# Channel mixing of two batches: six hidden blocks summed in a PSUM bank per addition, in place of three

## The chip, the cores and the metric

One NeuronCore of a Trainium2 chip runs the whole program; the other cores are idle. The metric is the device time of one execution in microseconds, median of the runs, smaller is better. TensorE (PE) multiplies into PSUM, VectorE (DVE) and ScalarE (ACT) read and write PSUM and SBUF, GpSimd (POOL) works on SBUF, and SyncE (SP) issues all DMA transfers.

## The reference

Attention over four batches of 448 rows with 12 heads of 64, then a mixer (over the rows, then over the channels), then a gated mixer. The change touches the channel mixing alone:

```python
x = attention(q, k, v)                                # (4, 448, 768)
xt = x.transpose(0, 2, 1)
u = x + (np.maximum(xt @ w_tok1, 0.0) @ w_tok2).transpose(0, 2, 1)
h2 = np.maximum(u @ w_ch1, 0.0) @ w_ch2               # 768 -> 1536 -> 768
x = u + h2
...
```

## The kernel before

Each product of fp32 precision is made of three matmuls on split operands (mm3, L332): each operand is a rounded high part and a low part, and high x high, high x low and low x high are summed in PSUM. Everything is transposed: U[b] holds channels on the partitions, in six blocks of 128 by 448 rows.

**What runs when.** Every instruction of the kernel is a job with an engine, a duration, a list of what it reads and writes and a priority. The class Plan (order, due, run; L134 to L270) plays the jobs through, engine by engine, six times with changing priorities, and the order of starts in the best pass is the order in which the program is written. Each engine then works strictly in that order. A change in one function can so move instructions of all others.

The attention of the 24 head pairs is in the front half: scores (L497, tile pss), masked reduction on DVE (L506), exponential on ACT (L523), normalisation on POOL (L544), transposes on PE (L581, pst), weighting (L683 and L688, pso); after each three pairs follows half a batch of row mixing (psm). The channel mixing of batches 0 and 1 is laid between these, from about 70 to 400 us; batches 2 and 3 are done in another way after 402 us (tile psf).

**The weights of channel mixing** arrive as 64-bit numbers. They are cut into 24 blocks, listed in UNITS: (1, f) is the part of w_ch1 that makes hidden block f of 128 channels, (2, q, e) the part of w_ch2 that takes hidden blocks 3q to 3q+2 to output blocks 2e and 2e+1. The place in this list is called position here, 0 to 23. convert (L375) loads a block into one of the way buffers (L381), narrows it on DVE in two halves of three steps each (narrow, L340; L351, L353, L355; tile psw), and stores it to DRAM as tile plain (L395). load_unit (L814) brings a block back (L818), casts its high part on ACT (L819) and makes the low part on POOL (lo_part, L327), in one of four buffers w0 to w3, by position modulo 4 (tile whl; the first three positions are split without the detour). Batch 1 loads the same 24 blocks again. The weights of the later gated mixer go the same way in tile gw (L1105, L1107), with the same narrowing steps on DVE.

**The two products.** ch1 (L831) takes a block of w_ch1: three jobs of six matmuls into a bank (tile ps, 18 matmuls), a relu on ACT (L843) into hid, and on DVE the remainder of the relu (relu_lo, L330), the low part of hid; this empties the bank. Six hid buffers h0 to h5 hold hidden blocks, by f modulo 6. ch2 (L846) takes a block of w_ch2: for each of its two output blocks, nine matmuls over three hidden blocks into a bank (tile ps again) and an addition of the bank into U on DVE (L859). Both products share two banks, 6 and 7 (banks_c, L791). In the program's order the tiles of both are told apart as ps1 and ps2.

Before the change the list runs: three of w_ch1, then four times three of w_ch1 (as long as there are any) and three of w_ch2. So a second product follows its hidden blocks with three other blocks between.

Of the kernel before, what the change touches and what calls it, by code (L numbers as in the profile page):

```python
# [16 lines left out]
B, H, S, D = 4, 12, 448, 64  # L17
# [6 lines left out]
NF = CH // 128  # L24
FF = 512
NG = FF // 128
HALF = 384
# [1 line left out]
MASKED = -8.0e9  # L29


UNITS = [(1, f) for f in range(3)]
for q in range(4):
    UNITS += [(1, f) for f in range(3 * q + 3, min(3 * q + 6, NF))] + [(2, q, e) for e in range(3)]
LN_EPS = 1e-6

DIRECT = tuple(range(3))
# [60 lines left out]
class Plan:  # L98
# [11 lines left out]
    def job(self, eng, us, emit, r=(), w=(), touch=(), prio=0.0, at=0.0, size=0, port=False, other=None):  # L110


        j = Job(eng, us, emit, prio, at, size, len(self.jobs), port, other)
        for k in r:
            if k in self.writer:
                j.before.add(self.writer[k])
            self.readers.setdefault(k, []).append(j)
        for k in w:
            if k in self.writer:
                j.before.add(self.writer[k])  # L120
            j.before.update(self.readers.get(k, ()))
            self.writer[k] = j
            self.readers[k] = []
        j.before.discard(j)
        for k in (*r, *w):
            if isinstance(k[0], Buf):
                j.bufs.add(k[0])
        for b in j.bufs:
            b.jobs.append(j)
        j.bufs |= set(touch)  # L130
        self.jobs.append(j)
        return j
# [146 lines left out]
def mixer_kernel(ctx: ExitStack, tc: tile.TileContext, qkv, wtok, wch, wgv, wsp, bsp, out):  # L279
# [19 lines left out]
    job = plan.job  # L299

    def buf(tag, shape, dtype, name):
        return plan.buf(tag, lambda t: sb.tile([128, *shape], dtype, tag=t, name=name))
# [6 lines left out]
    def bank(banks, name):  # L309
        return Buf(lambda i: psp.tile([128, 512], F32, tag=f"b{i}", name=name), None, banks=banks)  # L310
# [5 lines left out]
    def dve(n, psum=True):  # L316
        return (n * 1.05 + 60) / 1e3 if psum else (n * 1.09 + 40) / 1e3
# [14 lines left out]
    def mm3(ps, terms, first=True, last=True, **kw):  # L332

        n = len(terms)
        for i, (ah, al, bh, bl) in enumerate(terms):
            nc.tensor.matmul(ps, ah, bh, start=(first and i == 0), stop=False, **kw)  # L336
            nc.tensor.matmul(ps, ah, bl, start=False, stop=False, **kw)  # L337
            nc.tensor.matmul(ps, al, bh, start=False, stop=(last and i == n - 1), **kw)  # L338
# [63 lines left out]
    LOW = 1e5  # L402
# [147 lines left out]
    def u_keys(b, d):  # L550
        return [(U[b], d, 0), (U[b], d, 1)]
# [164 lines left out]
    mixed = {}  # L716
# [76 lines left out]
    WU = {}  # L793
# [28 lines left out]
    def split_u(b, ts, prio):  # L822
        u = U[b]
        for k in range(KM):
            t, i = ts[k // 3], k % 3
            job("ACT", act(S, False), lambda k=k, t=t, i=i: nc.scalar.copy(t.t[:, i, 0, :], u.t[:, k, :]), r=u_keys(b, k), w=[(t, i, 0)], prio=prio)
            job("POOL", pool(S), lambda k=k, t=t, i=i: lo_part(nc.gpsimd, t.t[:, i, 1, :], u.t[:, k, :], t.t[:, i, 0, :]), r=[*u_keys(b, k), (t, i, 0)], w=[(t, i, 1)], prio=prio)

    hidden = {}
# [14 lines left out]
        job("DVE", dve(S), lambda: relu_lo(h.t[:, 1, :], ps.t[:, :S], h.t[:, 0, :]), r=[(ps, 0), (h, 0)], w=[(h, 1)], prio=-1)  # L844

    def ch2(b, q, e, i):  # L846
        w = WU[b, i]
        u = U[b]
        hs = [hidden[b, 3 * q + f] for f in range(3)]
        for dd in range(2):  # L850
            d = 2 * e + dd
            ps = bank(banks_c, "ps2")

            def mms(dd=dd, ps=ps):
                cs = [slice(HALF * dd + 128 * f, HALF * dd + 128 * f + 128) for f in range(3)]
                mm3(ps.t[:, :S], [(w.t[:, 0, c], w.t[:, 1, c], h.t[:, 0, :], h.t[:, 1, :]) for c, h in zip(cs, hs)])

            job("PE", 1.82, mms, r=[*((w, 0, c) for c in range(2)), *((h, x) for h in hs for x in range(2))], w=[(ps, 0), ("mixed", b, d)], prio=LOW + 24 * b + i)
            job("DVE", dve(S), lambda d=d, ps=ps: nc.vector.tensor_tensor(u.t[:, d, :], ps.t[:, :S], u.t[:, d, :], op=ALU.add), r=[(ps, 0), *u_keys(b, d)], w=u_keys(b, d), prio=-1)  # L859

    def channel(b):
        xs = [buf(f"X{k}", [3, 2, S], F32R, "uhl") for k in range(2)]
        split_u(b, xs, -0.5)
        for i, u in enumerate(UNITS):
            if b:
                load_unit(b, i)
            if u[0] == 1:
                ch1(b, u[1], i, xs)
            else:
                ch2(b, u[1], u[2], i)  # L870

    everything = list(range(8))
# [167 lines left out]
    def channel_pair(b0, b1):  # L1040

        index = {u: i for i, u in enumerate(UNITS)}
        us = (U[b0], U[b1])
# [109 lines left out]
    for k in range(KM):  # L1153
        w, h, l = singles[k % 2], *value_w[k // 3 * 2 : k // 3 * 2 + 2]
        job("SP", 0.4, lambda k=k, w=w: nc.sync.dma_start(w.t, gated_w[8 + k]), r=[("gated", 8 + k)], w=[(w, 0)], prio=LOW + VALUE_PRIO + k, size=262144)
        job("ACT", act(FF, False), lambda k=k, w=w, h=h: nc.scalar.copy(h.t[:, k % 3, :], w.t), r=[(w, 0)], w=[(h, k, 0)], touch=[l], prio=LOW + VALUE_PRIO + k)  # L1156
        e, name, us = (nc.vector, "DVE", dve(FF, False)) if k in VALUE_DVE else (nc.gpsimd, "POOL", pool(FF))
# [122 lines left out]
    for i in range(2):  # L1280
        job("SP", 0.4, lambda i=i: nc.sync.dma_start(sp_in[i].t, wsp[:, 2 * S * i : 2 * S * i + 2 * S].rearrange("p (c s) -> p c s", c=2)), w=[(sp_in[i], 0)], prio=LOW + 130, size=458752)
        for c in range(2):
            w = sp_w[2 * i + c]
# [153 lines left out]
def _layout(inputs):  # L1437
# [34 lines left out]
    second = c2.reshape(4, 3, 128, 3, 2, 128).transpose(0, 3, 2, 4, 1, 5).reshape(4, 3, 128, DM)  # L1472
    wch = np.concatenate([first[u[1]] if u[0] == 1 else second[u[1], u[2]] for u in UNITS], axis=1)
    wi = inputs["moe2_w_in"]
# [33 lines left out]
```

## Time and profile before

| | us |
|---|---|
| median of 3 runs | 760.47 |
| the runs | 758.69, 760.47, 761.64 |
| span of the profiled execution | 760.7 |
| busy: PE, DVE, ACT, POOL | 747.2, 622.3, 427.4, 298.2 |
| chain that ended last: share of PE, of DVE | 9%, 2% |

The profiled execution's own time is given by its span alone; it stands 0.2 us over the median. The busy share of PE counts matmuls from their start to a modelled end; two that follow each other overlap, so the idle time of PE is what the table of waits shows, and the rate is seen in the starts of the timeline. The granted clock of PE is given per stretch, 1.00 for full speed.

### The profile page before, as it was taken

How to read it: one execution, taken by the hardware profiler on the slowest of the kernel's cores; microseconds unless marked ns; L12 is line 12 of the kernel's file. 1: busy time of each engine (PE TensorE's matmuls, PEld its weight loads, DVE VectorE, ACT ScalarE, POOL GpSimd, SP SyncE). 2: the span in 40 equal slices, each digit the busy share in tenths (PEclk: the TensorE clock that was granted, in tenths of full speed). 3: DMA queues.
4: the chain of work that ended last, by engine and by line, in shares of the span. 5: the costliest groups of instructions: out<-in, count | busy, mean ns of one | idle time of the engine just before them, and what ended most of it. 6: DMA issues, size and time to landing. Idle time of an engine off the chain costs nothing. (4 is left out here: it accounts for less than half of the span.)

```text
span 760.7 us, 12440 instructions
## 1 busy us (share of the span) xinstructions
PE 747.2 (98%) x4216; PEld 640.3 (84%) x4216; DVE 622.3 (82%) x1512; ACT 427.4 (56%) x1040; POOL 298.2 (39%) x354
## 2 busy tenths in 40 slices
PE   8999999999989999999999999999999999999998
PEld 4577778888887888888889989998988888888997
DVE  6999599999867878876469978999999897599482
ACT  6998776445347765552336666654573665545241
POOL 4788764265494766563310000000420151542210
PEclk9999999999999999999999999999999999999999
DMA  6687158999976898898823122520301100400213
GB/s 228 207 285 238 55 163 316 335 318 333 339 225 190 298 307 250 234 304 220 241 84 117 39 84 84 187 84 1 118 22 42 43 0 1 132 1 28 83 49 133
DMA packets 48608, 122.02 MB, mean 160 GB/s; under 512 B 4896, under 2 KB 20256, under 8 KB 48032
## 3 DMA queue, kind: packets, MB, share of 16 engines
q1 hardware_dynamic: 48544, 121.23, 48.7%
q8 instruction: 33, 0.54, 0.3%
q14 instruction: 31, 0.25, 0.1%
HBM read 91.46 MB, written 29.75 MB: 159 GB/s over the span
## 5 line engine op out<-in xcount | busy, mean ns | idle before, releaser
L336 PE MATMUL psf<-fb,fa 128*128 128x448 f32 x420 | 154.0, 367 | 1.2 <-DVE hs L1001 0.6
L337 PE MATMUL psf<-fb,fa 128*128 128x448 f32 x420 | 153.7, 366 | 0.0
L338 PE MATMUL psf<-fb,fa 128*128 128x448 f32 x420 | 153.6, 366 | 0.0
L327 POOL TENSOR_TENSOR whl<-whl 128x768 fp32r<-128x768 f32 x45 | 83.2, 1851 | 89.5 <-ACT whl L819 89.4
L523 ACT ACTIVATE P<-P,stats 128x448 f32<-128x448 f32 (+3 forms) x192 | 96.1, 505 | 31.1 <-DVE stats L506 30.8
L544 POOL TENSOR_SCALAR P<-P,stats 128x448 f32<-128x448 f32 (+3 forms) x192 | 88.3, 483 | 38.1 <-DVE stats L535 30.8
L336 PEld LDWEIGHTS psf<-fb,fa 128*128 128x128 f32 x420 | 78.9, 188 | 9.2 <-DVE hs L1001 1.0
L337 PEld LDWEIGHTS psf<-fb,fa 128*128 128x128 f32 x420 | 78.9, 188 | 6.8
L338 PEld LDWEIGHTS psf<-fb,fa 128*128 128x128 f32 x420 | 78.9, 188 | 6.7
L506 DVE CUSTOM_DVE_ANT_0 P<-pss,mask 128x448 f32<-128x448 f32 (+3 forms) x192 | 70.9, 415 | 16.4 <-PE pss L497 16.0
L938 ACT CAST fa<-raw 128x384 fp32r<-128x384 f32 (+1 forms) x112 | 56.4, 531 | 42.7 <-DVE raw L951 21.6
L327 POOL TENSOR_TENSOR wv<-wf,wv 128x512 fp32r<-128x512 f32 x6 | 9.2, 1546 | 153.2 <-ACT wv L1156 153.2
L327 DVE TENSOR_TENSOR fa<-raw,fa 128x384 fp32r<-128x384 f32 (+1 forms) x109 | 61.0, 585 | 7.1 <-ACT fa L938 7.1
L336 PE MATMUL ps<-hid,whl 128*128 128x448 f32 x144 | 55.2, 383 | 3.1 <-DVE hid L330 1.9
L819 ACT CAST whl<-whl 128x768 fp32r<-128x768 f32 x45 | 37.4, 833 | 34.6 <-DMA whl<-plain 33.5
L336 PE MATMUL ps<-uhl,whl 128*128 128x448 f32 x144 | 55.6, 386 | 0.2 <-DVE U L859 0.2
L338 PE MATMUL ps<-hid,whl 128*128 128x448 f32 x144 | 53.3, 370 | 0.0
L337 PE MATMUL ps<-hid,whl 128*128 128x448 f32 x144 | 53.3, 370 | 0.0
L338 PE MATMUL ps<-uhl,whl 128*128 128x448 f32 x144 | 52.7, 366 | 0.0
L337 PE MATMUL ps<-uhl,whl 128*128 128x448 f32 x144 | 52.7, 366 | 0.0
L859 DVE TENSOR_TENSOR U<-ps,U 128x448 f32<-128x448 f32 x48 | 29.5, 619 | 20.9 <-PE ps L338 20.8
L327 POOL TENSOR_TENSOR ql<-stage,qh 128x896 fp32r<-128x896 f32 x18 | 38.1, 2116 | 14.9 <-issue 11.7
(174 smaller groups left out, 1793.2 us busy)
## 6 DMA issues: line engine op xcount, KB each, us to landing
way<-in_wch SPq DMA_DIRECT2D x24, 768.0 KB, 5.7
whl<-plain SPq DMA_DIRECT2D x45, 384.0 KB, 5.0
stage<-in_qkv SPq DMA_DIRECT2D x23, 448.0 KB, 4.7
plain<-way SPq DMA_DIRECT2D x24, 384.0 KB, 6.7
raw<-plain SPq DMA_DIRECT2D x24, 384.0 KB, 3.9
round<-PB SPq DMA_DIRECT2D x7, 1024.0 KB, 6.2
PT<-round SPq DMA_DIRECT2D x28, 256.0 KB, 6.2
v<-in_qkv SPq DMA_DIRECT2D x24, 256.0 KB, 4.1
```

Source lines behind the costliest of these rows:

```text
L327: e.tensor_tensor(lo, x, hi.bitcast(F32), op=ALU.subtract)
L336: nc.tensor.matmul(ps, ah, bh, start=(first and i == 0), stop=False, **kw)
L337: nc.tensor.matmul(ps, ah, bl, start=False, stop=False, **kw)
L338: nc.tensor.matmul(ps, al, bh, start=False, stop=(last and i == n - 1), **kw)
L506: nc.vector.tensor_tensor_reduce(out=P(i)[:M, j, :], in0=ps(i, j), in1=mask[:M, S - 128 : S - 128 + W] if j == 0 and n < BLOCKS or M == 64 ...
L523: nc.scalar.activation(P(i)[:M, j, :], P(i)[:M, j, :], AF.Exp, bias=s.t[:M, 0, c : c + 1], scale=-1.0, accum_out=s.t[:M, 1, c : c + 1])
L544: nc.gpsimd.tensor_scalar(P(i)[:M, j, :], P(i)[:M, j, :], s.t[:M, 2, c : c + 1], 1.0, op0=ALU.mult, op1=ALU.mult)
L819: job("ACT", act(DM, False), lambda: nc.scalar.copy(w.t[:, 0, :], w.t[:, 1, :].bitcast(F32)), r=ks, w=ks, prio=p)
L859: job("DVE", dve(S), lambda d=d, ps=ps: nc.vector.tensor_tensor(u.t[:, d, :], ps.t[:, :S], u.t[:, d, :], op=ALU.add), r=[(ps, 0), *u_keys( ...
L938: job("ACT", act(n, False), lambda: nc.scalar.copy(part(o, 0), at(d)), r=[key(d)], w=[wk], prio=p + 0.1 * o)
```

## The change

The list now runs six of w_ch1, six of w_ch2, and the same again. Within the six of w_ch2 the blocks that serve the same output blocks stand in pairs: (2, 0, e) and (2, 1, e), then the next e. ch2 is called once for a pair and takes both weight blocks: a bank gets nine matmuls with the first block (hidden blocks 0 to 2 of the six) and nine with the second (hidden blocks 3 to 5), as two jobs, and one addition into U follows the eighteen. Per batch there are so 12 banks of 18 matmuls and 12 additions for the second product instead of 24 banks of nine and 24 additions. The host lays the blocks out in the new order. Batches 2 and 3 use the same blocks by another index and are otherwise as before.

```diff
-UNITS = [(1, f) for f in range(3)]
-for q in range(4):
-    UNITS += [(1, f) for f in range(3 * q + 3, min(3 * q + 6, NF))] + [(2, q, e) for e in range(3)]
+UNITS = []
+for x in range(2):
+    UNITS += [(1, f) for f in range(6 * x, 6 * x + 6)] + [(2, q, e) for e in range(3) for q in (2 * x, 2 * x + 1)]
...
     def ch2(b, q, e, i):
-        w = WU[b, i]
+        w = [WU[b, i - 1], WU[b, i]]
         u = U[b]
-        hs = [hidden[b, 3 * q + f] for f in range(3)]
         for dd in range(2):
             d = 2 * e + dd
             ps = bank(banks_c, "ps2")
...
+            for x in range(2):
+                hs = [hidden[b, 3 * (q - 1 + x) + f] for f in range(3)]
...
+                    mm3(ps.t[:, :S], [(w[x].t[:, 0, c], w[x].t[:, 1, c], h.t[:, 0, :], h.t[:, 1, :]) for c, h in zip(cs, hs)], first=x == 0, last=x == 1)
...
             job("DVE", dve(S), lambda d=d, ps=ps: nc.vector.tensor_tensor(u.t[:, d, :], ps.t[:, :S], u.t[:, d, :], op=ALU.add), r=[(ps, 0), *u_keys(b, d)], w=u_keys(b, d), prio=-1)
...
-            else:
+            elif u[1] % 2:
                 ch2(b, u[1], u[2], i)
```

The change moves instructions on every engine, since the plan is made anew. Two places show it. The first is VectorE ahead of the relu remainder of position 17 (the last of w_ch1 in both lists), whose bank is wanted by a second product of position 18. Before, from the second half of position 22 on (way2 holds even positions, way3 odd ones; psw is the bank that the narrowing steps share):

```order
L351 TENSOR_SCALAR psw_2636<-way2_156 128x384
L353 SCALAR_TENSOR_TENSOR psw_2636<-way2_156,psw_2636 128x384
L355 SCALAR_TENSOR_TENSOR way2_156<-way2_156,psw_2636 128x384
L330 SCALAR_TENSOR_TENSOR hid_2631<-ps1_2585,hid_2631 128x448
L351 TENSOR_SCALAR psw_2658<-way3_158 128x384
L353 SCALAR_TENSOR_TENSOR psw_2658<-way3_158,psw_2658 128x384
L355 SCALAR_TENSOR_TENSOR way3_158<-way3_158,psw_2658 128x384
L330 SCALAR_TENSOR_TENSOR hid_2677<-ps1_2622,hid_2677 128x448
```

And now, from the first half of position 21 on:

```order
L351 TENSOR_SCALAR psw_2487<-way3_158 128x384
L353 SCALAR_TENSOR_TENSOR psw_2487<-way3_158,psw_2487 128x384
L355 SCALAR_TENSOR_TENSOR way3_158<-way3_158,psw_2487 128x384
L330 SCALAR_TENSOR_TENSOR hid_2499<-ps1_2446,hid_2499 128x448
L351 TENSOR_SCALAR psw_2520<-gw_1948 128x384
L353 SCALAR_TENSOR_TENSOR psw_2520<-gw_1948,psw_2520 128x384
L355 SCALAR_TENSOR_TENSOR gw_1948<-gw_1948,psw_2520 128x384
L584 COPY PT_2518<-pst_2524 128x448
L351 TENSOR_SCALAR psw_2544<-way3_158 128x384
L353 SCALAR_TENSOR_TENSOR psw_2544<-way3_158,psw_2544 128x384
L355 SCALAR_TENSOR_TENSOR way3_158<-way3_158,psw_2544 128x384
L330 SCALAR_TENSOR_TENSOR hid_2558<-ps1_2490,hid_2558 128x448
```

The relu remainder of position 17 stood behind the first half of position 23; it now stands behind the second half of position 21.

The second place is TensorE, where a weight buffer is used up and the block four positions on is wanted. Before, the closest such places are positions 14 to 18: whl_2372 is position 14, whl_2561 is position 18 in the same buffer; shown are the last matmul on the one and the first matmuls of the others.

```order
L338 MATMUL ps2_2537<-hid_2012,whl_2372 128x448
...
L336 MATMUL ps1_2554<-uhl_864,whl_2427 128x448
...
L336 MATMUL ps1_2585<-uhl_864,whl_2489 128x448
...
L336 MATMUL ps1_2622<-uhl_864,whl_2516 128x448
...
L336 MATMUL ps2_2667<-hid_2285,whl_2561 128x448
```

Now it is positions 8 to 12: whl_1920 is position 8, whl_2006 position 9, whl_2077 and whl_2114 are 10 and 11, and whl_2184 is position 12, in the buffer of position 8. Shown are the last matmul on position 8 and the first of each nine that follow:

```order
L338 MATMUL ps2_2159<-hid_1703,whl_1920 128x448
L336 MATMUL ps2_2159<-hid_1825,whl_2006 128x448
...
L336 MATMUL ps2_2189<-hid_1458,whl_2077 128x448
...
L336 MATMUL ps2_2189<-hid_1825,whl_2114 128x448
...
L336 MATMUL ps2_2222<-hid_1458,whl_2077 128x448
...
L336 MATMUL ps2_2222<-hid_1825,whl_2114 128x448
...
L336 MATMUL ps1_2257<-uhl_864,whl_2184 128x448
```

Between the last use of a buffer and the first use of the block that follows in it stood three blocks of 18 matmuls; at this place now stand five times nine.

## Rows read from the trace of the kernel before

**Rows 1.** The page's head and part 1: busy us (share of the span) xinstructions

```profile
span 760.7 us, 12440 instructions
...
PE 747.2 (98%) x4216; PEld 640.3 (84%) x4216; DVE 622.3 (82%) x1512; ACT 427.4 (56%) x1040; POOL 298.2 (39%) x354
```

**Rows 2.** Table of waits, TensorE: us in total, times, longest us

```profile
PE ps L336 <- DVE hid L330: 1.9, 1, 1.9
...
PE ps L336 <- DVE U L859: 1.2, 2, 1.1
```

**Rows 3.** Table by stretch: length, busy us (xinstructions) by engine, PE clock, DMA share, GB/s

```profile
180.00:200.00 20.00, 18.68 (x96) 16.02 (x95) 18.39 (x44) 7.69 (x18) 8.07 (x7) 1.00 0.94 332
200.00:220.00 20.00, 18.07 (x84) 16.28 (x83) 14.49 (x31) 10.55 (x19) 14.90 (x15) 0.91 0.85 287
...
214.00:216.00 2.00, 2.00 (x7) 1.76 (x7) 1.93 (x5) 1.88 (x4) 2.00 (x3) 0.50 0.57 219
```

**Rows 4.** Timeline of TensorE, 192 to 217 us: start, us, instruction [idle before <-releaser]

```profile
194.91 0.47 PE L336 MATMUL ps<-hid,whl 128*128 128x448 f32 x1 [1.05 <-DVE U L859]
...
212.13 0.47 PE L336 MATMUL ps<-hid,whl 128*128 128x448 f32 x1 [1.94 <-DVE hid L330]
...
213.04 0.51 PE L337 MATMUL ps<-hid,whl 128*128 128x448 f32 x1
...
216.63 0.36 PE L338 MATMUL ps<-hid,whl 128*128 128x448 f32 x1
216.83 0.36 PE L336 MATMUL ps<-hid,whl 128*128 128x448 f32 x1
```

**Rows 5.** Timeline of VectorE, 192 to 212 us

```profile
192.58 0.56 DVE L351 TENSOR_SCALAR psw<-gw 128x384 uint32<-128x384 uint32 x1 [0.92 <-DMA gw<-in_wgv]
...
194.24 0.62 DVE L859 TENSOR_TENSOR U<-ps,U 128x448 f32<-128x448 f32 x1
...
209.07 0.56 DVE L351 TENSOR_SCALAR psw<-way 128x384 uint32<-128x384 uint32 x1 [1.15 <-DMA way<-in_wch]
...
210.98 0.56 DVE L355 SCALAR_TENSOR_TENSOR way<-way,psw 128x384 uint32<-128x384 uint32 x1 [0.75 <-DMA plain<-way]
211.45 0.62 DVE L330 SCALAR_TENSOR_TENSOR hid<-ps,hid 128x448 fp32r<-128x448 f32 x1
```

**Rows 6.** VectorE by line, 100 to 215 us: xcount | busy us, mean ns | idle before

```profile
L353 DVE SCALAR_TENSOR_TENSOR psw<-way,psw 128x384 uint32<-128x384 uint32 x38 | 21.3, 561 | 1.2
...
L506 DVE CUSTOM_DVE_ANT_0 P<-pss,mask 128x192 f32<-128x192 f32 (+3 forms) x33 | 12.6, 413 | 0.1
L859 DVE TENSOR_TENSOR U<-ps,U 128x448 f32<-128x448 f32 x13 | 7.8, 616 | 0.0
```

**Rows 7.** Timeline of TensorE, 94 to 103 us: half a score, weighting, transposes

```profile
94.80 0.47 PE L497 MATMUL pss<-qh 64*128 64x448 f32 x2
...
95.75 0.85 PE L741 MATMUL psm<-ident,U 128*64 128x128 f32 x6
...
100.10 0.97 PE L683 MATMUL pso<-PT,v 128*64 128x448 f32 x4
...
102.32 0.66 PE L581 MATMUL pst<-ident,P 128*128 128x128 f32 x4
```

**Rows 8.** Timeline of SyncE's queue: block loads of positions 12, 18 and 20

```profile
164.36 0.32 SPq L818 DMA_DIRECT2D whl<-plain  x1
...
197.44 0.38 SPq L818 DMA_DIRECT2D whl<-plain  x1
...
204.81 0.32 SPq L818 DMA_DIRECT2D whl<-plain  x1
```

**Rows 9.** Timeline of GpSimd: splits of positions 12, 18, and 20 with 21

```profile
171.00 1.85 POOL L327 TENSOR_TENSOR whl<-whl 128x768 fp32r<-128x768 f32 x1
...
206.47 1.86 POOL L327 TENSOR_TENSOR whl<-whl 128x768 fp32r<-128x768 f32 x1
...
215.32 3.63 POOL L327 TENSOR_TENSOR whl<-whl 128x768 fp32r<-128x768 f32 x2
```

More of the change, by code (lines that the diff above doesn't have):

```diff
@@ L852, in ch2, with mms @@
             ps = bank(banks_c, "ps2")
[L854 to L858, printed above, removed]
+            for x in range(2):
+                hs = [hidden[b, 3 * (q - 1 + x) + f] for f in range(3)]
+                def mms(dd=dd, ps=ps, x=x, hs=hs):
+                    cs = [slice(HALF * dd + 128 * f, HALF * dd + 128 * f + 128) for f in range(3)]
+                    mm3(ps.t[:, :S], [(w[x].t[:, 0, c], w[x].t[:, 1, c], h.t[:, 0, :], h.t[:, 1, :]) for c, h in zip(cs, hs)], first=x == 0, last=x == 1)
+                job("PE", 1.82, mms, r=[*((w[x], 0, c) for c in range(2)), *((h, y) for h in hs for y in range(2))], w=[(ps, 0), ("mixed", b, d)], prio=LOW + 24 * b + i)
             job("DVE", dve(S), lambda d=d, ps=ps: nc.vector.tensor_tensor(u.t[:, d, :], ps.t[:, :S], u.t[:, d, :], op=ALU.add), r=[(ps, 0), *u_keys(b, d)], w=u_keys(b, d), prio=-1)
```

## The prediction

> **What bounds the kernel now.** The page's first part comes first: the span and the busy share of each engine [rows 1]. TensorE is busy 747.2 of 760.7 us, so there is little to win anywhere: a change that leaves the number of matmuls alone can only move the 13.5 us in which TensorE stands still, and what its clock loses. This change leaves all 864 matmuls of channel mixing for batches 0 and 1 in place. The second view is the table of waits for TensorE alone [rows 2]: two of its three longest entries are in channel mixing (tile ps), 1.9 us for VectorE's hid and 1.2 us for VectorE's U (the other stands at the kernel's start, which the change leaves alone). The third view is the table by stretch [rows 3]: both lie between 180 and 220 us, where TensorE is busy 18.68 and 18.07 of 20 us, and from 200 to 220 us its granted clock averages 0.91. Nothing else in the middle of the kernel stands out.
>
> The timeline of TensorE shows the two places [rows 4]. At 194.91 a second product begins 1.05 us late, behind an addition (L859) on VectorE. At 212.13 the next one begins 1.94 us late, behind the relu remainder (L330). Neither waits for its own operands: both need one of the two PSUM banks of channel mixing, which VectorE has not emptied yet. VectorE's timeline says why [rows 5]. At 192.58 VectorE had stood idle 0.92 us for a load of gw, with the addition that frees the bank three instructions behind it. At 209.07 it had stood 1.15 us for a load of way, at 210.98 another 0.75 us for a store of plain, and the relu remainder that frees the bank (211.45) is the very next instruction. So the cause is the order on VectorE: narrowing of weights that has not arrived sits ahead of the instruction that frees a bank, and a bank that is filled in nine matmuls leaves only nine matmuls of time.
>
> **What one such wait costs.** A matmul's row ends 0.36 us after its start while the next starts 0.20 us after it (the rows at 216.63 and 216.83 [rows 4]), so a wait costs 0.16 us more than the idle time shown. Idle time in channel mixing there: 1.05 at 194.91, 1.94 at 212.13, and about 0.2 for the rest of the 1.2 us that rows 2 put down to U: 3.2 us in three waits, with 3 x 0.16 = 0.5 it is 3.7 us. After the longest of them the matmuls get slower: from 213.04 to 216.63 ten of them take 3.59 us instead of 10 x 0.203 = 2.03 us [rows 4], which is the dip of the granted clock in rows 3: 0.50 from 214 to 216 us, the lower of its two levels, 1.2 GHz. That adds 1.6 us. The whole place costs 5.3 us.
>
> **The change part by part.** *Additions.* 48 additions into U become 24: 24 x 0.616 us = 14.8 us less on VectorE [rows 6]. By itself this is worth nothing, because VectorE is not what ends; it counts only through what stands behind an addition in VectorE's order.
>
> *Time to empty a bank.* A bank of the second product is filled by 18 matmuls (3.7 us) in place of 9 (1.83 us). Where the order runs bank after bank, VectorE has twice the time for the other one. Where both banks are open at once (positions 18 to 21 of batch 0) the first is closed nine matmuls ahead of the second, so the margin is that of before, 1.83 us plus what attention puts between.
>
> *VectorE's order at the place of the long wait.* In both kernels it follows position 17, the last block of the first product. Ahead of its relu remainder VectorE now has 6 additions instead of 12 (6 x 0.62 = 3.7 us less), three narrowed half blocks less (each three steps of 0.56 us [rows 6], some 0.55 to 0.6 from start to start: 5.0 us) and one attention score block of 8 masked reductions less (8 x 0.38 = 3.1 us by the group's 12.6 us over 33 [rows 6]), with the small steps around it about 12.8 us less in all. TensorE reaches the place earlier as well: one pair's scores, four transposes and the weighting of one pair are now behind it, which by their rows is 2 x 0.95 + 0.4 + 2.2 = 4.5 us [rows 7]; I count 4.8 with the change of kind between them. VectorE's lead over TensorE therefore grows by 12.8 - 4.8 = 8 us, against a wait of 1.94 us. The narrowing steps ahead of it belong to position 21, no longer to 22 and 23, and the load of position 21 stands on SP right behind the block load of position 17, which waits until position 13 is used up, some 20 us of matmuls ahead of this place. Summed along both orders with the durations of this trace, the lead of the freeing instruction over the matmul that needs the bank is smallest at this very place before (4.8 us, and 5.2 to 5.8 around the other two waits); afterwards it is nowhere under 11 us. I take all three waits as gone: 760.7 - 3.7 - 1.6 = 755.4 us.
>
> *Weight buffers.* This is the term that speaks against the change. Four buffers hold the split weight blocks, and a second product now needs two at once. A buffer can be loaded again when its block is used up, and the new block must be loaded (SP), cast (ScalarE) and split (GpSimd) before its turn. Before, the shortest such interval is 54 matmuls, 11.0 us (positions 16 to 19). Now it is 45 matmuls, 9.2 us, at position 12, and 10.4 us at position 14. What the way takes is read from load issue to the end of the split: position 12 of before 164.36 to 172.85, 8.5 us; position 18 197.44 to 208.33, 10.9 us [rows 8, 9]. Bounds for the new wait: nothing by the first, 10.9 - 9.2 = 1.7 us by the second. The tight place now falls near 165 to 175 us, close to the first row, but the blocks from position 8 to 14 are now used within 25.6 us of matmuls instead of 31.7. I take 0.7 us, nearer to the lower end; both ends go into the range.
>
> *Start of the second product.* It now needs six hidden blocks. The first nine matmuls of each bank read the first three, so the last relu is covered by 1.83 us or more in all four places; nothing for it, and if that cover were gone it would cost one relu remainder, 0.6 us. Later stages have the same instructions; nothing.
>
> **Sum.** 755.4 + 0.7 = 756.1 us, I say 756.2. The profiled span (760.7) stands 0.2 us over the median of the runs shown (760.47), so no shift is needed; the runs lie between 758.69 and 761.64, about 1.5 us to either side. What a measurement here can tell from no change is about 0.5%, 3.8 us: faster means under 756.7, slower over 764.3.
>
> **Rivals.** *The wait moves.* VectorE still takes narrowing in order, so a late load may hold some other instruction, for instance the masked reductions of the attention block that now falls among positions 19 to 21. Price: one wait as the largest in the trace with its slow clock, 1.94 + 0.16 + 1.6 = 3.7 us, giving 755.4 + 3.7 = 759.1 us. For it: SP's order still mixes loads for narrowing with loads that wait for a buffer. Against it: VectorE's lead grows everywhere.
>
> *The banks stay the limit.* In this trace every one of the three waits is for a bank that VectorE still holds [rows 4, 5]; if holding a bank longer is what hurts, the waits stay, nothing is won, and the time is 760.7 us. Against it: the late instruction is late by VectorE's order, and the bank's margin doubles. The Trainium skill speaks for this rival: "PSUM — Partial Sum Buffer", in its summary of rules for kernel authors, asks to evacuate a bank promptly since PSUM is small, and here each of two banks is held for twice as many matmuls. By that rule the 5.3 us stay; by the rows they go. I give it one chance in ten.
>
> *Slower: the ring of four weight buffers runs dry.* Place: positions 10 to 15 of batch 0, where the new intervals are 13.5, 11.6, 9.2, 12.2, 10.4 and 13.4 us. Condition: loads that leave in pairs slow each other so that the way takes as long as the longest of the busy stretch, position 20 of before, 204.81 to about 217.2 (the first of the two splits from 215.32), 12.4 us [rows 8, 9]. Then TensorE waits 0.8 + 3.2 + 0.2 + 2.0 = 6.2 us, two of these waits are long enough for a clock dip of 1.6 us each, and the time is 755.4 + 6.2 + 3.1 = 764.7 us. It decides from a way of 9.2 us on, and eats the whole gain from about 11.6 us. For it: ways of 10.9 and 12.4 us exist in this trace. Against it: they fall where narrowing loads, stores and attention loads crowd the DMA queues, and the attention loads leave this stretch.
>
> **How the numbers follow.** The forecast has 0.53, the moved wait 0.25, the banks 0.10, the dry ring 0.12. The forecast's own range is 754 to 758: 755.4 less the spread of the runs, and 755.4 + 1.7 with some of it. With the moved wait and the banks the range reaches to 762; only the dry ring and stray cases lie outside. Of the forecast some 0.72 lies under 756.7, which with a little of the moved wait gives 0.42 for faster. Half of the dry ring and some of the rest lies over 764.3: 0.10 for slower. The rest, 0.48, is no change that can be told.
>
> **What would show it.** Right: between 180 and 220 us TensorE is busy 19.5 of 20 us or more at a granted clock of 1.00, the wait of ps for hid and U falls under 0.5 us in TensorE's table, and the additions into U count 24. Wrong: a wait of ps for whl (GpSimd's split) near 165 to 185 us would show the ring; a wait of pst or pss of a microsecond or more, or another dip of the clock, the moved wait; the same waits on hid and U, the banks.

## The result, and the profile after

The changed kernel takes 764.46 us (median of 9 runs, 761.81 to 766.35), the kernel before in the same session 760.00 (9 runs, 757.56 to 761.64). The ratio is 1.0057, with a 95% interval of 1.0038 to 1.0076: slower, by about as much as can be told from no change. In a later session, with 12 runs of the changed kernel (its order written out, as told below) and 29 of the one before, it was 762.79 against 760.03, a ratio of 1.0031 (1.0017 to 1.0046). The forecast of 756.2 us was wrong, and the range of 754 to 762 did not hold the time.

The head and part 1 of the page after (busy us, share of the span, instructions) answer to [rows 1]:

```profile
span 760.0 us, 12396 instructions
...
PE 748.3 (98%) x4216; PEld 639.7 (84%) x4216; DVE 610.0 (80%) x1488; ACT 428.6 (56%) x1040; POOL 296.3 (39%) x354
```

The span is 0.7 us shorter than that of before, while the median is longer. Two things lie in this. The profiled execution of after took 761.81 us, the fastest of its nine. And every run's time is its span plus 1.8 us: 761.81 for a span of 760.0, 763.41 for 761.6, 758.60 for 756.8. So the profiled execution of before, with a span of 760.7, was one of about 762.5 us, slower than each of the three runs that the prediction set it beside.

The table by stretch of the changed kernel (length; busy us and instructions of PE, PEld, DVE, ACT, POOL; clock of PE; share of the DMA engines; GB/s) answers to [rows 3]:

```profile
160.00:180.00 20.00, 19.98 (x99) 18.16 (x98) 18.16 (x35) 4.00 (x6) 8.29 (x5) 1.00 0.96 343
180.00:200.00 20.00, 20.00 (x114) 17.64 (x114) 18.14 (x44) 12.91 (x29) 15.24 (x15) 1.00 0.92 326
200.00:220.00 20.00, 18.95 (x129) 15.20 (x129) 18.10 (x47) 11.00 (x25) 16.09 (x18) 1.00 0.95 304
220.00:240.00 20.00, 19.45 (x136) 15.07 (x133) 17.02 (x51) 16.84 (x47) 19.19 (x23) 1.00 0.72 218
360.00:380.00 20.00, 19.19 (x107) 16.51 (x106) 4.57 (x8) 6.89 (x11) 6.76 (x4) 1.00 0.82 248
```

What was forecast for 180 to 200 us is there: TensorE is busy 20.00 us where it was busy 18.68, and the granted clock is 1.00 in every stretch shown. But 200 to 240 us now lacks 1.6 us, and 360 to 380 us lacks 0.8, where nothing had stood out. The table of waits for TensorE (us in total, times, longest) answers to [rows 2]:

```profile
PE pso L683 <- ACT PT L585: 1.2, 2, 0.9
...
PE psv L336 <- ACT v L1190: 0.8, 1, 0.8
...
PE ps L336 <- DVE U L860: 0.8, 1, 0.8
...
PE pst L581 <- DVE xs L327: 0.4, 1, 0.4
```

The wait for hid is gone in this trace (in that of the order written out, below, 0.4 us of it is back, at 204 us). In its place stand four waits that the forecast did not have: two in attention (pso at 218 us, pst at 229), one for a bank (ps for U at 375), and one in the later gated mixer (psv at 586). Nowhere does ps wait for whl, a weight block.

**The weight ring.** Position 12 was the tightest place of the forecast. SyncE's queue issues its block load at 165.26:

```profile
165.26 0.32 SPq L818 DMA_DIRECT2D whl<-plain  x1
```

GpSimd's timeline has its split, which ends at 173.79:

```profile
171.93 1.86 POOL L327 TENSOR_TENSOR whl<-whl 128x768 fp32r<-128x768 f32 x1 [4.79 <-ACT whl L819]
```

And in TensorE's timeline this is the first matmul on the block:

```profile
174.16 0.36 PE L336 MATMUL ps<-uhl,whl 128*128 128x448 f32 x1
```

The way took 8.5 us, the very number taken from before, and the block was ready 0.4 us ahead of its use. So the ring ran, but with nothing in hand.

**Where attention waits.** ScalarE's timeline of the changed kernel, 213 to 219 us (start, us, instruction, and in brackets the idle time before it and what ended it):

```profile
213.85 1.02 ACT L585 COPY PT<-pst 128x448 f32<-128x448 f32 x2
217.79 0.84 ACT L819 CAST whl<-whl 128x768 fp32r<-128x768 f32 x1 [2.92 <-DMA whl<-plain]
218.54 1.06 ACT L585 COPY PT<-pst 128x512 f32<-128x512 f32 x2
```

And TensorE's, at the same place:

```profile
218.47 0.27 PE L497 MATMUL pss<-qh,ql 64*128 64x192 f32 x2
219.65 0.60 PE L683 MATMUL pso<-PT,v 128*64 128x448 f32 x2 [0.91 <-ACT PT L585]
```

ScalarE stands 2.92 us before the cast of a weight block whose load is late. The copies of attention's transposed weights are the next instruction in its order, and TensorE waits 0.91 us for them. The late block itself is in time for its matmuls; what is late is what stands behind its cast.

**The two other waits** are in TensorE's timeline at 375 and 586 us:

```profile
374.86 0.37 PE L338 MATMUL ps<-hid,whl 128*128 128x448 f32 x1
376.04 0.44 PE L336 MATMUL ps<-hid,whl 128*128 128x448 f32 x1 [0.81 <-DVE U L860]
...
585.73 0.37 PE L338 MATMUL psf<-fb,fa 128*128 128x448 f32 x1
586.91 0.50 PE L336 MATMUL psv<-wv,fb 128*128 128x512 f32 x1 [0.82 <-ACT v L1190]
```

At 375 us the plan lets the pair of positions 20 and 21 of batch 1 begin in the bank that was closed last (the matmul at 374.86 closes it), while the other bank has been closed nine matmuls longer. So TensorE waits for the whole addition, although VectorE is idle. At 586 us ScalarE's copy of psv stands behind a square root and a gate in ScalarE's order:

```profile
585.27 0.20 ACT L1198 ACTIVATE bias<-bias 128x1 f32<-128x1 f32 x1 [1.53 <-DVE bias L1195]
585.80 0.58 ACT L1004 ACTIVATE gate<-gate 128x448 f32<-128x448 f32 x1 [0.33 <-DVE gate L1002]
586.28 0.58 ACT L1190 ACTIVATE v<-psv 128x512 f32<-128x512 f32 x1
```

With the 0.16 us per wait of [rows 4], these two cost 0.97 and 0.98 us, in each of the three traces of the changed kernel (the two here and that of the order written out).

### The profile page after: what moved, and what is told of

The parts are those of the page before. It is cut to its first block, busy times and chain, and to the rows that moved or that the text cites. A ratio compares the mean times of both kernels' runs of the same rounds, so it can differ in the third digit from the quotient of the medians.

```text
span 760.0 us, 12396 instructions
## 1 busy us (share of the span) xinstructions
PE 748.3 (98%) x4216; PEld 639.7 (84%) x4216; DVE 610.0 (80%) x1488; ACT 428.6 (56%) x1040; POOL 296.3 (39%) x354
## 5 line engine op out<-in xcount | busy, mean ns | idle before, releaser
L544 POOL TENSOR_SCALAR P<-P,stats 128x448 f32<-128x448 f32 (+2 forms) x192 | 87.6, 478 | 46.3 <-DVE stats L535 37.7
L336 PE MATMUL ps<-hid,whl 128*128 128x448 f32 x144 | 54.7, 380 | 0.9 <-DVE U L860 0.8
L338 PE MATMUL ps<-hid,whl 128*128 128x448 f32 x144 | 52.7, 366 | 0.0
L337 PE MATMUL ps<-hid,whl 128*128 128x448 f32 x144 | 52.7, 366 | 0.0
L324 POOL TENSOR_SCALAR xsh<-fb 128x64 fp32r<-128x64 f32 x24 | 17.4, 744 | 62.5 <-PE psv L338 36.0
L581 PE MATMUL pst<-ident,P 128*128 128x128 f32 x272 | 39.1, 277 | 2.5 <-POOL P L544 0.8
```

The lines of the kernel that those rows point to most:

```text
L324: nc.gpsimd.tensor_scalar(hi, x, 1.0, 1.0, op0=ALU.mult, op1=ALU.mult)
L544: nc.gpsimd.tensor_scalar(P(i)[:M, j, :], P(i)[:M, j, :], s.t[:M, 2, c : c + 1], 1.0, op0=ALU.mult, op1=ALU.mult)
L581: nc.tensor.transpose(ps.t[:, c : c + 128], src, ident)
```

## The experiments

### Both kernels again

The same two kernels, each run and traced once more.

> The changed kernel once more, for a second trace, since the first one is of its fastest execution (761.8 us of 761.8 to 766.4). Theory ring: weight blocks of positions 9 to 20 come only 0.4 to 2.8 us ahead of their use in the first trace, so an execution with slower transfers shows TensorE waiting for whl (the split on GpSimd) by 2 us or more between 160 and 215 us. Theory attention: the waits are of pso and pst between 205 and 235 us, as the 0.9 us and 0.4 us of the first trace, only longer (2 to 5 us with a clock dip). Time expected: 763 to 766 us.

> The kernel before once more, for a second trace. Its span in the trace that the prediction used was 760.7 us; the spans of the changed kernel's executions are 1.8 us under their times, so that execution took about 762.5 us, above every run shown. Expected: 757.5 to 761 us, and between 180 and 220 us less than the 5.3 us of waits and clock loss that the prediction took for typical: 0 to 3 us.

The changed kernel took 763.41 us (span 761.6) and the kernel before 761.09 (span 759.3). The changed one again had the waits at 230, 376 and 587 us and none for whl, but not the 0.91 us of pso at 218: from 200 to 220 us TensorE lost 0.35 us. The 1.6 us by which it was longer than in its first trace it had lost before the first channel matmul (71.47 us, against 69.25). The kernel before, table by stretch and table of waits:

```profile
180.00:200.00 20.00, 19.78 (x101) 16.96 (x100) 18.92 (x45) 7.44 (x18) 7.87 (x5) 1.00 0.98 337
200.00:220.00 20.00, 18.79 (x91) 16.21 (x90) 15.79 (x33) 10.60 (x20) 16.12 (x16) 1.00 0.89 314
```

```profile
PE ps L336 <- DVE hid L330: 1.0, 2, 0.6
...
PE ps L336 <- DVE U L859: 0.4, 2, 0.2
```

The same waits stand at the same place, but 1.4 us in all instead of 3.1, and with the full clock. The trace that the forecast was made from was one of the slower executions of the kernel before.

### The order without the merged additions, and the merged additions in another order

First, the new list of six and six, with ch2 as before: one block, nine matmuls and one addition per bank, 24 banks per batch. Second, the changed kernel, in which both banks of a pair get their nine matmuls with the first block before the second block begins. Both are planned anew.

```diff
-        w = [WU[b, i - 1], WU[b, i]]
+        w = WU[b, i]
...
-            elif u[1] % 2:
+            else:
```

```diff
-        for dd in range(2):
-            d = 2 * e + dd
-            ps = bank(banks_c, "ps2")
-            for x in range(2):
+        pss = [bank(banks_c, "ps2") for _ in range(2)]
+        for x in range(2):
+            for dd in range(2):
+                d, ps = 2 * e + dd, pss[dd]
```

> The new list of blocks, but each block of the second product with banks of nine matmuls and its own two additions, as before: 48 additions. A weight buffer is used up block by block again, so the shortest interval in the ring is about 11 us. Theory ring: faster than the changed kernel, 759 to 762 us. Theory attention (the list moves attention late, whatever the additions do): as slow as the changed kernel or slower, 764 to 768 us.

> The changed kernel, but of each pair the first block fills nine matmuls of both banks before the second block is used, so that every weight buffer is free again two steps of nine after its first use; 24 additions as changed. Theory ring: the waits for weights go, 758 to 761 us. Theory attention: no better than the changed kernel, 763 to 766 us, with the same waits of pso and pst.

The order alone: 761.41 us against 759.84, ratio 1.0013 (0.9992 to 1.0034): no difference that can be told. Its trace has the wait of 0.81 us at 375 too, so that wait does not need the merged additions; it also has 0.4 us of ps for whl, at 280 us, the one wait for a weight block that any table of waits shows. Block by block: 758.03 us, ratio 0.9977 (0.9959 to 0.9995), faster than the kernel before and some 5 us faster than the changed one. So summing a bank over six blocks need not make the kernel slower; how a pair is laid out, and what plan comes of it, can turn the sign. But each of these is another plan of the whole program, so they do not say which of its waits matter.

### One order held fixed, one thing cut at a time

From here on the order of instructions, the banks and the choice of engines of the changed kernel are written out as the planner gave them, and single things are edited in that. The edits: nothing; cast and split of a weight block on 128 of 768 columns; three pairs block by block; loads of 64-bit weights cut to a twelfth.

```diff
-nc.scalar.copy(w.t[:, 0, :], w.t[:, 1, :].bitcast(F32))
+nc.scalar.copy(w.t[:, 0, :128], w.t[:, 1, :128].bitcast(F32))
...
-lo_part(nc.gpsimd, w.t[:, 1, :], w.t[:, 1, :].bitcast(F32), w.t[:, 0, :])
+lo_part(nc.gpsimd, w.t[:, 1, :128], w.t[:, 1, :128].bitcast(F32), w.t[:, 0, :128])
```

```diff
-nc.sync.dma_start(b.t[:, : 2 * n], src.bitcast(U32))
+m = 64 if keep is not None and keep > 5 else n
+nc.sync.dma_start(b.t[:, : 2 * m], src[:, :m].bitcast(U32))
```

> The changed kernel itself, with the order of its instructions, its banks and its choice of engines written out as the planner gave them, so that the next three can be edits of one and the same order. All theories: the same time as the changed kernel, 763 to 765 us. Its two traced executions so far (spans 760.0 and 761.6) were among its fastest; this third one should show where a slower one loses 2 to 4 us more. The dry ring (four weight buffers, slack of 0.4 to 4.8 us at positions 9 to 20 in the trace): a wait of ps for whl in a slower execution. Fixed waits (one microsecond each in the plan's order, at 218, 229, 375 and 586 us): the same waits again and nothing else.

> The order of the changed kernel, with the cast and the split of every weight block cut from 768 to 128 columns, and all weight operands read from these 128 columns (the products are then of other numbers; every matmul stays as long). The way of a block becomes shorter by (0.83 - 0.2) + (1.84 - 0.35), some 2.1 us, so each slack on the ring grows by that. Dry ring: the median falls by 2 to 4 us against the changed kernel, to 760 to 762. Fixed waits: no change, 763 to 765.

> The order of the changed kernel, with one edit in TensorE's order: in the three pairs of positions 6 to 11 of batch 0, which run bank by bank (A first block, A second, B first, B second), both banks get their first nine matmuls before the second block begins (A first, B first, A second, B second). VectorE's additions stay where they were but for one step. The first block of a pair is so used up nine matmuls (1.83 us) earlier and the second is wanted nine later: slack 1.8 us more at positions 9 to 12 and 14. Dry ring: 1 to 3 us less than the changed kernel, 761 to 763. Fixed waits: no change, 763 to 765. Banks held too long (both open at once for longer): a wait of ps for U of up to a microsecond per pair, 764 to 767.

> The order of the changed kernel, with the loads of the 64-bit weights for narrowing cut to a twelfth from position 6 on (the rest of a buffer keeps older weights, so the products are of other numbers). This takes traffic off the DMA queues between 60 and 200 us and makes these loads land early; block loads, cast and split stay. Late narrowing or crowded queues as the cause: the median falls by 2 to 4 us against the changed kernel, to 760 to 762, and the block loads of positions 9 to 16, 5.5 to 8 us in the trace, get shorter. Fixed waits: no change, 763 to 765.

| kernel | median us | runs | lowest to highest | ratio to before (95%) |
|---|---|---|---|---|
| before | 760.03 | 29 | 757.98 to 763.53 | |
| changed, order written out | 762.79 | 12 | 760.76 to 764.46 | 1.0031 (1.0017 to 1.0046) |
| short way of a block | 760.69 | 12 | 759.10 to 762.73 | 1.0006 (0.9992 to 1.0020) |
| three pairs block by block | 768.71 | 6 | 766.76 to 769.76 | 1.0105 (1.0083 to 1.0127) |
| small loads of 64-bit weights | 759.91 | 12 | 759.26 to 761.04 | 0.9993 (0.9979 to 1.0007) |

The small loads take 2.9 us off, and the runs lie in 1.8 us instead of 3.7. The short way, which leaves all loads as they are, takes 2.1 us off; it also gives ScalarE and GpSimd less to do, so it does not tell the lateness of a block from the time that its cast and split take. The stretches say where it comes from. The changed kernel, order written out:

```profile
180.00:200.00 20.00, 19.66 (x110) 17.28 (x110) 17.59 (x43) 12.87 (x30) 14.73 (x14) 1.00 0.92 315
200.00:220.00 20.00, 18.72 (x124) 15.20 (x124) 17.57 (x40) 10.66 (x24) 16.29 (x19) 1.00 0.93 305
220.00:240.00 20.00, 19.42 (x146) 14.99 (x143) 18.14 (x57) 16.76 (x45) 19.20 (x23) 1.00 0.77 230
```

With the short way:

```profile
180.00:200.00 20.00, 19.77 (x111) 17.51 (x111) 17.96 (x46) 10.05 (x30) 9.91 (x15) 1.00 0.94 332
200.00:220.00 20.00, 20.00 (x139) 16.38 (x140) 17.80 (x45) 10.85 (x28) 12.18 (x18) 1.00 0.93 320
220.00:240.00 20.00, 20.00 (x145) 16.54 (x142) 17.47 (x57) 15.72 (x52) 14.85 (x22) 1.00 0.80 235
```

With the small loads:

```profile
180.00:200.00 20.00, 20.00 (x116) 17.79 (x115) 17.40 (x43) 13.12 (x30) 14.84 (x15) 1.00 0.66 209
200.00:220.00 20.00, 19.86 (x137) 15.78 (x137) 18.20 (x47) 12.50 (x28) 18.48 (x19) 1.00 0.77 245
220.00:240.00 20.00, 20.00 (x142) 16.48 (x139) 18.17 (x53) 16.46 (x51) 18.99 (x23) 1.00 0.78 228
```

From 180 to 240 us TensorE's idle time is 2.2 us in the changed kernel, 0.2 with the short way, 0.1 with the small loads. The waits at 375 and 586 us stay in both. So late weights, with the casts and splits that follow them, cost this kernel 2 to 3 us, at the place where they cost the kernel before, and in none of its traces does TensorE wait for a weight block. The table of DMA issues from 130 to 200 us (KB each, median us from issue to landing) shows how late a load is: in the changed kernel's first trace

```profile
way<-in_wch SPq DMA_DIRECT2D x11, 768.0 KB, 6.7
whl<-plain SPq DMA_DIRECT2D x12, 384.0 KB, 6.8
```

and with the small loads

```profile
whl<-plain SPq DMA_DIRECT2D x13, 384.0 KB, 3.4
...
way<-in_wch SPq DMA_DIRECT2D x11, 64.0 KB, 3.2
```

The three pairs block by block lie above every range expected, by my own edit; the wait of ps for U that came is the one foreseen for banks held too long, only longer. The additions stayed where they had been in VectorE's order, while the bank closes 1.83 us of matmuls later. VectorE then stood 3.57 us for it, its narrowing was late, and the next addition came 2.6 us late for TensorE. VectorE's timeline:

```profile
166.87 0.62 DVE L860 TENSOR_TENSOR U<-ps,U 128x448 f32<-128x448 f32 x1 [3.57 <-PE ps L338]
...
172.44 0.62 DVE L860 TENSOR_TENSOR U<-ps,U 128x448 f32<-128x448 f32 x1
```

TensorE's:

```profile
173.11 0.47 PE L336 MATMUL ps<-hid,whl 128*128 128x448 f32 x1 [2.63 <-DVE U L860]
```

So this run says nothing on the ring, but it prices a bank that is closed later than VectorE's order expects: 6 us for three pairs.

### Is it ScalarE, and what do late loads cost the kernel before?

Three runs: in the order written out, ScalarE casts from a constant in batch 0 and no longer waits for a load; the kernel before with the small loads; and the order written out with the banks exchanged at 375 us.

```diff
-nc.scalar.copy(w.t[:, 0, :], w.t[:, 1, :].bitcast(F32))
+nc.scalar.copy(w.t[:, 0, :], w.t[:, 1, :].bitcast(F32) if b else mask)
```

> The order of the changed kernel, as written out. In batch 0 ScalarE casts the high part of a weight block from a constant tile instead of from the block that was loaded (so the weights there are other numbers), and no longer waits for the load; GpSimd's split still waits for it, so TensorE gets a block exactly as late as before. Theory: ScalarE stands in its own order before a cast whose block load is late (2.9 us at 212 in the second trace of the changed kernel, 2.9 us at 217 in the first), and the exponentials and copies of attention that are queued behind the cast make TensorE wait (0.9 us each time, in pst or pso). Then the waits of pst, pso and pss at 180 to 240 us fall to half or less and the median falls by 1.5 to 2.5 us, to 760.3 to 761.3. Rival: TensorE waits for weight blocks themselves, or GpSimd is the one that holds attention up: no change, 762 to 764.

> The kernel before, with one edit: the loads of the 64-bit weights for narrowing cut to a twelfth from position 6 on (the rest of a buffer keeps older weights, so the products are of other numbers), as in the earlier run on the changed kernel, which took 2.9 us off that. The plan stays the same. Theory: VectorE's wait for these loads, with the instruction that frees a bank behind it, is what the kernel before loses between 180 and 220 us (1 to 4 us in its two traces); the waits of ps for hid and U there go, and the median falls by 2 to 4 us, to 756 to 758. Then the changed order is about 3 us worse than the old one even when no load is late. Rival: the bank waits come from the nine matmuls of a bank alone: ps still waits for hid or U by a microsecond or more, 759 to 760.5.

> The order of the changed kernel, as written out, with the two banks of channel mixing exchanged from the pair of positions 20 and 21 of batch 1 on. There the plan lets a pair begin in the bank that was closed last (TensorE waits 0.81 us for the addition at 375 us, in all traces of the changed kernel) while the other one has been free for nine matmuls. Theory: the wait at 375 goes and nothing else, 0.8 to 1.0 us less than the changed kernel, 761.8 to 762.0. Rival: the wait only moves to the next addition: no change, 762.8.

The kernel before took 760.37 us beside these runs. **The kernel before with small loads** took 757.46 (757.06 to 759.14), ratio 0.9960 (0.9945 to 0.9975): 2.9 us less, as the theory said. Its waits of ps for hid and U are down to at most 0.2 us, and its stretches read

```profile
180.00:200.00 20.00, 19.78 (x102) 17.04 (x101) 19.13 (x47) 7.62 (x19) 9.53 (x5) 1.00 0.82 255
200.00:220.00 20.00, 19.81 (x101) 17.84 (x100) 16.81 (x35) 10.86 (x20) 15.68 (x16) 1.00 0.73 221
```

**The cast from elsewhere** took 762.57 (1.0024, 1.0005 to 1.0043), 0.2 us less than the changed kernel, where 1.5 to 2.5 had been expected. In its trace (span 759.1) the largest wait from 180 to 240 us is 0.35 us, and TensorE stands 0.9 us there in all, against 1.1 to 2.8 us in the five traces of this order that keep their loads and casts. In three of these the largest wait is for a copy on ScalarE behind a late cast: 0.91 us at 219 us, 0.91 at 215 (the order written out; its cast stood 2.91 us for the load) and 1.23 at 221 (the other bank; 3.23 us). So ScalarE is one that holds TensorE there, but the median did not follow: set against the kernel before of each session the gain is 0.6 us, and the two intervals rule out neither no gain nor one of 1.5 us. GpSimd still waits for the same loads with attention's normalisation behind its split, and VectorE for its own with everything else behind; a later trace shows TensorE waiting 0.64 us for GpSimd (below). My theory was too narrow: the lateness costs, and the traces show it leaving by more than one queue; in what shares, no run shows.

**The other bank** took 761.94 (1.0010, 0.9991 to 1.0029), 0.85 us less than the changed kernel, as expected though within the uncertainty; its trace has no wait at 375 us.

### The two fixed waits taken out, and the variant again

In the order written out, the banks as in the last run, and one copy moved in ScalarE's order:

```diff
+L1190 ACTIVATE v<-psv 128x512
 L1198 ACTIVATE bias<-bias 128x1
 L1004 ACTIVATE gate<-gate 128x448
-L1190 ACTIVATE v<-psv 128x512
```

> The order of the changed kernel, as written out, with two edits: the banks exchanged from positions 20 and 21 of batch 1 on, as in the last run, and one copy of psv on ScalarE moved ahead of the square root and the gate that stood in front of it (586 us; TensorE waits 0.82 us there in every trace). Theory: these are two fixed waits of about 1 us each: 2 us less than the changed kernel (762.8), 760.8, which is the time of the kernel before. Rival: what is won there is lost to the next wait: 762 to 763.

> The same two edits, and the loads of the 64-bit weights cut to a twelfth from position 6 on (products of other numbers). Theory: the new order without late loads took 759.9, so 2 us less: 757.9, within 0.5 us of the old order without late loads (757.5). Then nothing else of the new order costs anything. Rival, the thin ring: it stays at 759 or above.

> The variant that gives both banks their nine matmuls with the first block before the second block begins (planned anew, 758.0 when it ran), with the loads of the 64-bit weights cut to a twelfth from position 6 on (products of other numbers). If its gain is that late loads hurt it less: hardly any change, 757 to 758. If it only has a luckier order: 2 to 3 us less, 755 to 756.

> The variant that runs a pair block by block, again, for a tighter interval: 758.0 us, ratio to the kernel before 0.997 to 0.999. If it was luck of that session: 760.

The kernel before took 760.66 us beside these runs. Both waits out: 761.64 (1.0013, 0.9993 to 1.0033), so 1.0 us over the kernel before where the changed kernel stood 2.8 over it. TensorE's timeline shows that only the first wait was won whole; the second came back in part at the next product of its kind (the wait at 597 us, behind VectorE), and at 228 us attention waits for GpSimd:

```profile
228.82 0.55 PE L581 MATMUL pst<-ident,P 128*128 128x128 f32 x3 [0.64 <-POOL P L544]
...
597.06 0.50 PE L336 MATMUL psv<-wv,xsh 128*128 128x512 f32 x1 [0.56 <-DVE gate L1002]
```

The same with small loads: 758.92 (0.9982, 0.9967 to 0.9997), 1.0 us less than with small loads alone, not the 2 that were expected, and 1.2 us more than the old order with small loads when each is taken against its session's kernel before (-1.74 and -2.91 us; the two intervals overlap, so its size is rough). TensorE's timeline of this run has two waits that the trace of the old order with small loads has not:

```profile
239.61 0.63 PE L582 MATMUL pst<-ident,P 128*128 128x128 f32 x4 [0.46 <-DVE xs L327]
...
594.14 0.50 PE L336 MATMUL psv<-wv,xsh 128*128 128x512 f32 x1 [0.56 <-DVE gate L1003]
```

With 0.16 us for each they come to 1.3 us, about the size of that remainder. No run takes them out, so that they are the remainder is not shown.

The variant block by block again took 758.68 (0.9967, 0.9947 to 0.9987), the same advantage as before; with small loads 756.99 (0.9954, 0.9939 to 0.9969), 1.7 us less. So it too loses something to late loads, though less than the other two orders, 2.9 each. The later of its two traces, of the fastest of twelve executions (756.86 us), has no stretch from 160 to 240 us with less than 20.00 us busy (the earlier one, of 758.60 us, lacks 0.9 us from 180 to 220):

```profile
180.00:200.00 20.00, 20.00 (x119) 16.99 (x118) 17.83 (x37) 9.13 (x18) 12.66 (x13) 1.00 0.97 334
200.00:220.00 20.00, 20.00 (x116) 17.92 (x115) 18.11 (x47) 14.98 (x36) 17.86 (x18) 1.00 0.84 293
220.00:240.00 20.00, 20.00 (x149) 16.28 (x150) 16.33 (x48) 14.48 (x35) 19.03 (x24) 1.00 0.70 218
```

It beats both kernels: some 2 us, 0.2 to 0.3%, under the kernel before, with intervals that leave out 1.

## Why the prediction was wrong, step by step

**Right in the main: the three bank waits go, and the dip of the clock with them.** In the first trace TensorE is busy 20.00 us from 180 to 200, the granted clock is 1.00 (2.4 GHz) from 160 to 240, and ps no longer waits for hid; in three later traces of this order 0.3 to 0.6 us of that wait is back. Of the signs named, the 24 additions came (48 before); 19.5 of 20 us busy came from 180 to 200 but not from 200 to 220 (18.95 us), because of attention. The cause was read rightly too: the kernel before with small loads loses these waits (0.2 us is left), and nothing but those loads was changed in it. The Trainium skill's "PSUM — Partial Sum Buffer", in its summary for kernel authors, asks to evacuate a bank promptly. That rule did not decide here: with banks held for 18 matmuls the waits got shorter, and the largest bank wait of channel mixing that is left (0.81 us) comes from a choice between two banks.

**Wrong: the price of what goes, and the base it was taken from.** "The profiled span (760.7) stands 0.2 us over the median of the runs shown (760.47), so no shift is needed" was the first failed step. Time is span plus 1.8 us, so that execution stood 2.0 us over the median and its 5.3 us of waits were not the usual ones. Its 755.4 us of span without them is 757.2 us of time. The second trace of the kernel before shows 1.4 us of idle time in them and no loss of clock; all that late loads cost the kernel before is 2.9 us at the median. The target without them was 757.5, not 755.4.

**Wrong: "Weight buffers", the term of 0.7 us.** The way was the 8.5 us of the lower bound, the block was ready 0.4 us ahead, and as TensorE's wait for a block the term was even too large: it is nil in each trace of the changed kernel. The step that failed was to ask only when TensorE would want the block. A late block load first holds ScalarE's cast and GpSimd's split, and what stands behind these in the same queues is attention: ScalarE stood 2.92 us for a load, and TensorE 0.91 us for the copy behind its cast. The text names what is queued behind a late load for VectorE alone. What share each queue has stays open: the cast taken from elsewhere won back 0.2 us, the short way 2.1 us. Late loads cost the changed kernel 2.9 us (762.79 to 759.91), as much as they had cost the kernel before (760.37 to 757.46). So late loads cost as much as ever: what was won at the banks was lost again, and the waits that the traces of the changed order show in that stretch are mostly in attention.

**Wrong: "Later stages have the same instructions; nothing", and "the margin is that of before".** A new plan moves the order of every stage. It put a pair on the bank closed last (0.97 us) and a copy behind a gate (0.98 us). Taking both out brought 1.0 to 1.8 us. With them out and no late loads, the new order still takes about 1.2 us more than the old one; two waits of its trace (0.46 and 0.56 us, behind VectorE) are of that size, but the remainder is open.

**The sum as measured**, against the kernel before: late loads, 2.9 us in either kernel, 0 net; fixed waits, 1.0 to 1.8 us; remainder, about 1.2 us. That is 2.2 to 3.0 us, for 2.8 measured in the later session (4.5 in the first, whose interval overlaps). The remainder is found by subtraction, so the sum must close. Nor do the 2.9 us of the kernel before all lie at the banks: each of its two traces also has two waits of 0.5 to 0.6 us between 450 and 560 us, behind VectorE, that its trace with small loads has not.

**The rivals.** "The wait moves" was right in kind, with attention named as the one that would be held, though by VectorE, and by a single wait; from the right base, 757.5 + 3.7, it would have said 761.2. "The ring runs dry" gave 764.7, within 0.3 us of the result, and that is luck: no trace of the changed kernel shows its mechanism, a wait for whl with a dip of the clock. "The banks stay the limit" fell. The first sign given for the moved wait, "a wait of pst or pss of a microsecond", is nearly what came: 0.91 us, of pso in one trace and of pst in another.

## What to carry to other kernels

Set a profiled execution's time, not its span, beside the median, and take a second trace before a stall of 2 us in it is priced as the usual one. Where a load feeds a helper engine, ask what stands behind the waiting instruction on that engine as well as who wants its result: here late loads cost 2.9 us while no matmul waited for a weight block. And where a planner lays out the whole program, an edit in one stage is an edit in all; hold the order fixed to learn what the edit does, and judge two layouts of the same edit before the idea itself, since here one was 0.3 to 0.6% slower and the other 0.2 to 0.3% faster.

## What was not expected of the hardware

From 130 to 200 us a load of 384 KB took 6.8 us from issue to landing (median of 12) in the changed kernel, whose DMA engines were 0.94 busy there, and 3.4 us (median of 13) with small loads, at 0.69 busy. The share alone does not set it: in the two traces of the kernel before, the same loads took 5.3 and 5.5 us at 0.95 and 0.97 busy. With the smaller traffic the scatter from run to run fell too: from 3.7 to 1.8 us in the changed kernel's order (12 runs each), from 5.6 to 2.1 us in the old one (29 runs from 757.98 to 763.53, and only 12 from 757.06 to 759.14). So in this kernel part of what looks like noise of the measurement is transfers that land late.
